# Attention with recurrent memory plus a GELU layer: weight copies kept in PSUM, and the order of VectorE's work in a segment

## Chip, cores and metric

The kernel runs on one core of one Trainium2 chip, as one program. The metric is device time in microseconds of one execution; a lower time is better. Engines are named as in the profile: PE is TensorE, PEld its weight loads, DVE is VectorE, ACT is ScalarE, POOL is GpSimd, and SP is SyncE, which issues most DMAs.

## What is computed

`x` is 2048 tokens of 1024 elements in bf16. After a layer norm it goes two ways, and the output is the sum of x and both:

```python
xn = layernorm(x)
# A: 64 segments of 32 tokens, one after the other, 32 heads of 128, 8 memory rows
for s in range(64):
    h = concat(mem, xn[32*s : 32*s+32])                    # 40 rows
    q, k, v = h @ Wq, h @ Wk, h @ Wv                       # 1024 x 4096 each
    p = softmax(where(mask, q @ k.T / sqrt(128), -1e9))    # per head
    o = (p @ v) @ Wo                                       # 4096 x 1024
    mem, out_A[s] = o[:8], o[8:]
# B: out_B = gelu(xn @ w1 + b1) @ w2 + b2                  # 1024 x 3584 x 1024
out = x + out_A + out_B
```

The mask is causal inside a segment; the 8 memory rows see all and are seen by all. Each segment needs the memory of the one before, so the 64 segments of A are a chain.

## The kernel before

**First stage (lines 293 to 605).** The layer norm and all of B, for four blocks of 512 tokens. During the last block's second product (the loop at line 584) the weights of A are loaded over the weights of B, place by place as each is used for the last time. All these loads are in SP's queue, in program order: an issue that waits for its place holds up those behind it. The line before the last of the stage fetches `xt2` and `xt3`, which must wait until that block's result has been stored from there (line 412); after it stands the load of one half of a Wo unit into `d_oL` (line 605). The other half went into `half_home` early (line 573).

**Second stage (line 612 on).** The weights of A are cut into 64 units of 128 x 2048 bf16 (512 KB): K, Q, V have two halves of eight units each, Wo has sixteen. 46 stay in SBUF for good. 18 must come anew in each segment, through six places (`start_stream`, line 240): when PE has finished a streamed unit (`unit_done`, line 674), the next one in a fixed order is started into its place. 16 of the 18 come by DMA from a packed copy (one of them 384 KB only, with the rest fixed in `part_home`). Two, `IN_PSUM` (the fifth unit of Q's first half) and `IN_BANKS` (the last streamed unit of Wo), are kept in four PSUM banks called `kept`, and DVE copies them out, two banks to a unit (line 247). `keep` (line 647) puts them there once, in segment 0: PE transposes a 128 x 128 block, DVE or ACT copies the result to SBUF, and PE transposes it back into the bank. It uses the bank `mixed` in between.

A segment runs the passes K half 0, Q half 0, K half 1, Q half 1, V half 0, V half 1 (`half_pass`, line 732; eight units, each four matmuls side by side) and then sixteen Wo units (`o_product`). The list `at` puts other work behind a unit of a pass. `scores(u)` (line 808) multiplies queries and keys of half u into the bank `mixed`, ACT takes exponentials, and DVE applies the mask with two minima (line 833). `sums(u)` (line 836) adds the rows up with PE, again in `mixed`; ACT takes a logarithm and two exponentials (lines 852, 855), and DVE makes the weights `pd_main` and `pd_left` (lines 862, 866). `values(u)` multiplies by V. In `turn_q` ACT copies a pass's result to SBUF (line 758) and DVE transposes 32 x 32 blocks (line 772); DVE's order is the order of the program.

**Left rows.** Only memory and the first 24 tokens of a segment go through the passes as its own. The last 8 tokens of four segments are collected in one block of 32 "left" rows. A group's left block is multiplied by one half after another while those units are at hand: by a segment's place in its group of four, left products run in K half 1 and V half 0 (place 0), Q half 0 (place 1), Q half 1 (place 2), K half 0 and V half 1 (place 3), each for the group then beginning or next; Wo's for one place in four. Up to six units of the next left product are made at the end of the segment before. `turn_kL`, `turn_qL`, `left_values` take these results out of PSUM: a copy by DVE, and for K and Q a transpose.
`q_left(u)` (line 788) copies 8 left queries of each head into the block that `scores` reads, from `qL` or, at place 2 and 3 (half 0) and place 3 (half 1), from a piece of the bank `mixed` (`qS`), where `keep_q(u)` (line 798) has saved them at place 1 and 2 before `qL` is overwritten. The masks lie in `mixed` too.

**Banks.** Results of passes, of left products, of `values` and of Wo share three PSUM banks. `new_acc` takes the one that has been free for longest, and PE's first write into it waits for whoever read it last.

Of the kernel before, what the change touches and what calls it, by code (L numbers as in the profile page):

```python
# [10 lines left out]
BF16 = mybir.dt.bfloat16  # L11
U32 = mybir.dt.uint32
F32 = mybir.dt.float32
# [4 lines left out]
P = 128  # L18
# [68 lines left out]
def kernel(  # L87
# [149 lines left out]
    stream_tiles, slot_of = {}, {}  # L237
    used = 0

    def start_stream(slot):  # L240
        if not starts:
            return
        n = starts.popleft()
        unit, t = streams[n], slab(slot)
        if unit in kept_in:
            for c0, bank in kept_in[unit]:
                nc.vector.tensor_copy(out=t[:, c0:c0 + 1024], in_=bank)  # L247
# [45 lines left out]
    with tc.tile_pool(name="ma", bufs=2) as ma, tc.tile_pool(name="mps", bufs=6, space=PSUM) as mps:  # L293
# [191 lines left out]
        for tg in range(4):  # L485
# [46 lines left out]
            if not last:  # L532
                xnT = new_xnT(tg + 1)
                for t in range(4):
                    xtoks[4 * tg + 4 + t] = load_x(4 * tg + 4 + t)
                if tg == 0:
                    for unit, c in copies.items():
                        fetch(c, unit)
                    fetch_resident(*low)
                for t in range(4):  # L540
                    ln_stats(4 * tg + 4 + t, xtoks[4 * tg + 4 + t])
                ln_sqrt(4 * tg + 4, 4 * tg + 8)
                ln_rstd(4 * tg + 4, 4 * tg + 8)
                for t in range(4):
                    ttg = 4 * tg + t
                    xn = ln_apply(ttg + 4)
                    rsb = xtoks[ttg]
                    for nb in range(2):
                        cs = slice(nb * 512, (nb + 1) * 512)
                        ps = mps.tile([P, 512], F32, name="ps")  # L550
                        for fc in range(FC):
                            nc.tensor.matmul(  # L552
                                ps[:, :],
                                lhsT=gts[fc // 4][:, fc % 4, t * P:(t + 1) * P],
                                rhs=w2_sb[fc // 2][:, fc % 2, cs],
                                start=(fc == 0),
                                stop=(fc == FC - 1),
                            )
                        nc.vector.tensor_tensor(out=ps[:, :], in0=ps[:, :], in1=b2bc[:, cs], op=ALU.add)
                        nc.vector.tensor_tensor(out=rsb[:, cs], in0=ps[:, :], in1=rsb[:, cs], op=ALU.add)  # L560
                        if nb == 1:
                            turn_x(ttg + 4, xn, xnT)
                    keep_R(ttg, rsb)
                keep_xT(tg + 1, xnT)
                for t in range(4):
                    turn_R(4 * tg + t)
            else:


                for slot in RING:  # L570
                    start_stream(slot)
                h = 4 * IN_BANKS[1] + 2 * IN_BANKS[2]
                nc.sync.dma_start(out=half_home[:, :], in_=Wo_v[:, h, :])
                fetch_resident(*(place for place in RES_PLACES if place.startswith("w1_")))
                put_mem(o_sb, nxt["hT"], mps.tile([P, 512], F32, name="ps"))
                pss = [mps.tile([P, 512], F32, name="ps") for _ in range(6)]
                pss += [mps.tile([P, 512], F32, name="pT", bufs=2) for _ in range(2)]
                for n in range(8):
                    cs = slice((n % 2) * 512, (n % 2 + 1) * 512)
                    nc.tensor.matmul(pss[n][:, :], lhsT=ones[0:1, :], rhs=b2row[0:1, cs], start=True, stop=False)  # L580
                    nc.tensor.matmul(
                        pss[n][:, :], lhsT=ident, rhs=xtoks[4 * tg + n // 2][:, cs], start=False, stop=False
                    )
                for fc in range(FC):
                    for t in range(4):
                        for nb in range(2):
                            nc.tensor.matmul(  # L587
                                pss[2 * t + nb][:, :],
                                lhsT=gts[fc // 4][:, fc % 4, t * P:(t + 1) * P],
                                rhs=w2_sb[fc // 2][:, fc % 2, nb * 512:nb * 512 + 512],  # L590
                                start=False,
                                stop=(fc == FC - 1),
                            )
                    if fc % 2:
                        fetch_resident(f"w2_{fc // 2}")
                    if fc % 4 == 3:
                        fetch_resident(f"gT{fc // 4}")
                for n in range(8):
                    cs = slice((n % 2) * 512, (n % 2 + 1) * 512)
                    cp = nc.scalar.copy if n % 2 else nc.vector.tensor_copy  # L600
                    cp(out=xtoks[4 * tg + n // 2][:, cs], in_=pss[n][:, :])
                for t in range(4):
                    keep_R(4 * tg + t, xtoks[4 * tg + t])
                fetch_resident("xt2", "xt3")
                nc.sync.dma_start(out=d_oL[:, :], in_=Wo_v[:, h + 1, :])

# [5 lines left out]
    with tc.tile_pool(name="late", bufs=1) as late, \  # L612
# [25 lines left out]
        masks_at = there[:, 32 * NL:32 * NL + NX + GRP * 16]  # L638
        mask_order = masks_at[:, 0:NX]
        mask_left = masks_at[:, NX:].rearrange("p (g q) -> p g q", g=GRP)  # L640
        kept = banks.tile([P, 4, 1024], BF16, name="kept")

        def copy_bits(out, in_):

            nc.vector.tensor_single_scalar(out=out, in_=in_, scalar=0, op=ALU.bitwise_or)

        def keep(unit, c0, w, bank):

            turned = [late.tile([P, 512], BF16, name=f"VL{n}").rearrange("p (k t) -> p k t", k=4) for n in range(2)]
            for n in range(2):  # L650
                for k in range(4):
                    nc.tensor.transpose(trs[n][:, k, :], w[:, 512 * n + P * k:512 * n + P * (k + 1)], ident)
                (nc.scalar.copy if n else nc.vector.tensor_copy)(out=turned[n], in_=trs[n])
            for n in range(2):
                for k in range(4):
                    c1 = 512 * n + P * k
                    nc.tensor.transpose(kept[:, bank, c1:c1 + P], turned[n][:, k, :], ident)
            kept_in.setdefault(unit, []).append((c0, kept[:, bank, :]))

        def unit_tile(unit):  # L660
# [29 lines left out]
        for s in range(NSEG):  # L690
# [87 lines left out]
            def turn_kL(ps, u):  # L778
                kL[u] = sp.tile([P, 16, 32], BF16, name=f"kL{u}")
                turn(ps, kL[u][:, :, :], nc.vector.tensor_copy)  # L780
# [133 lines left out]
                        )  # L914


            psK, psKL = half_pass("K", 0, left_k[0], {})
            turn_k(psK, 0)
            if first:
                turn_kL(psKL, 0)  # L920
            psQ, psQL = half_pass("Q", 0, left_q[0], {})
            if first:
                keep(IN_BANKS, 1024, d_oL, 2)
                keep(IN_BANKS, 0, half_home, 3)
                nc.sync.dma_start(out=part_home, in_=Wo_v[:, 4 * PART[1] + 2 * PART[2], 0:PART_COLS])
                copy_bits(mixed[:, 468:512].bitcast(U32), mask.bitcast(U32))
                for t in outs:
                    nc.vector.memset(t[:, :, 0:32], 0.0)
                turn_qL(psQL, 0)
            q_left(0)  # L930
            turn_q(psQ)
            if left_q[0] and not first:
                keep_q(0)
                turn_qL(psQL, 0)
            psK1, psK1L = half_pass("K", 1, left_k[1], {})
            st["kT", 1] = nat_home
            rows_out(psK1, nat_home, nc.scalar.copy)
            at = {
                0: [lambda: scores(0), lambda: nc.vector.transpose(out=nat_home, in_=nat_home)],
                7: [lambda: sums(0)],  # L940
            }
            if left_k[1]:
                at[1] = [lambda: turn_kL(psK1L, 1)]
            elif left_k[0]:
                at[1] = [lambda: turn_kL(psKL, 0)]
            psQ1, psQ1L = half_pass("Q", 1, left_q[1], at)
            if first:
                turn_qL(psQ1L, 1)
            q_left(1)
            turn_q(psQ1)  # L950
            if left_q[1] and not first:
                keep_q(1)
                turn_qL(psQ1L, 1)
            psV, psVL = half_pass("V", 0, left_v[0], {})
            st["V", 0] = values_out(psV, sp.tile([P, 512], BF16, name="v", tag="a"), nc.scalar.copy)
# [27 lines left out]
            else:  # L983
                at = {5: [lambda: values(1, (0, 1))]}
            if left_v[1] and not first:
                at[6].append(lambda: left_values(1, psV1L))
            at.setdefault(0, []).append(load_res)
            psX = new_acc()
            for n, unit in enumerate(O_UNITS):
# [103 lines left out]
```

## Time and profile before

| what | value |
|---|---|
| four runs | 1893.39, 1894.7, 1905.26, 1908.27 us; median 1899.98 |
| the profiled execution | 1908.27 us, of which the span from first to last instruction is 1906.6 |
| PE, DVE, ACT, POOL busy | 91%, 48%, 33%, 14% |
| segment 0 begins, ends | 423.4 us (first product of K), 466.0 us (copy of its Wo result, line 1002) |
| segments 1 to 63 | 466.0 to about 1890 us, 22.6 us each |
| HBM read over the span | 599.39 MB |

The page's times are those of one execution, so sums are made against 1908.27 us. "Idle before" in a group's line is the time its engine stood still just ahead of it, with who ended that. A matmul's end is modelled, so a gap read between two matmuls is some 0.2 us shorter than the pause in issuing them. In a view by windows the columns are the stretch, its length, each engine's busy time, PE's granted clock, the mean busy share of the DMA engines (it can exceed 1 a little, since packets of one engine overlap) and GB/s.

### The profile page before, as it was taken

Reading aid. Unit: us, or ns where it says so; the run is one execution under the profiler, and the core shown is the slowest. Engines: PE = TensorE matmul, PEld = TensorE weight load, DVE = VectorE, ACT = ScalarE, POOL = GpSimd, SP = SyncE. Lnnn points to the kernel's source line nnn. Section 1 sums busy time; section 2 is a strip of 40 time slices with the busy share of each in tenths; the row PEclk is TensorE's granted clock in tenths of the full one; section 3 lists DMA queues with packets and bytes.
Section 4 is the critical chain, followed back from the end, with each engine's and each line's share of the span. In section 5 each row is a group of like instructions: output and inputs, shape, how many; then the busy total and the mean of one; then the engine's idle time right before and its main releaser. Section 6 shows DMA issues by size and latency. Waiting matters only on the chain.

```text
span 1906.6 us, 72995 instructions
## 1 busy us (share of the span) xinstructions
PE 1737.0 (91%) x32255; PEld 944.9 (50%) x32275; DVE 921.7 (48%) x2222; ACT 637.0 (33%) x1356; POOL 276.1 (14%) x538
## 2 busy tenths in 40 slices
PE   7999999997899899999989889989899999999887
PEld 3444444444454555545445545454555455555454
DVE  6657574604444444444444444444445444444443
ACT  5334342402333333333323333333333333333332
POOL 0000000001341111211112111112111111111211
PEclk9999999999999999999999999999999999999999
DMA  9821211588999999999999999999999999999997
GB/s 335 265 52 44 55 45 52 189 327 315 399 388 387 364 380 391 383 377 397 374 378 371 382 366 370 378 368 380 372 397 378 385 385 385 361 369 386 369 369 303
DMA packets 220025, 618.39 MB, mean 324 GB/s; under 512 B 47243, under 2 KB 65595, under 8 KB 219708
## 3 DMA queue, kind: packets, MB, share of 16 engines
q1 hardware_dynamic: 199292, 593.57, 82.3%
q0 software_dynamic: 16320, 17.52, 2.8%
q8 instruction: 252, 4.13, 0.8%
q10 hardware_dynamic: 4096, 2.64, 0.4%
q14 instruction: 65, 0.53, 0.1%
HBM read 599.39 MB, written 30.34 MB: 330 GB/s over the span
## 4 chain that ended last, share of the span: by engine, by line
PE 67%; DMA 19%; DVE 6%; issue 4%; ACT 3%; POOL 0%; DVEq 0%; ACTq 0%; POOLq 0%; SPq 0%
PE acc L714 32%; PE ps L503 10%; DMA u<-Wc_K 10%; PE acc L907 9%; PE ps L552 8%; DMA u<-Wc_O 5%; PE ps L587 2%; DMA u<-Wc_Q 2%; PE acc L881 2%; ACT mixed L855 2%; DVE b_oL L772 1%; DMA outL_d<-half_home 1%; DVE pd_main L862 1%; PE mixed L816 1%; DMA u<-Wc_V 1%
## 5 line engine op out<-in xcount | busy, mean ns | idle before, releaser
L714 PE MATMUL acc<-u,hr_home 128*32 128x512 bf16 x11520 | 784.5, 382 | 36.3 <-DMA u<-Wc_K 14.3
L714 PEld LDWEIGHTS <-hr_home 128*32 128x32 bf16 x12288 | 354.7, 97 | 326.5 <-issue 77.8
L714 PE MATMUL acc<-u,hrL 128*32 128x512 bf16 x2880 | 260.2, 380 | 17.4 <-issue 9.6
L503 PE MATMUL ps<-u 128*128 128x512 bf16 x896 | 196.4, 382 | 2.6 <-ACT u L387 2.6
L907 PE MATMUL acc<-u,d_oL 128*32 128x256 bf16 (+1 forms) x3552 | 177.1, 290 | 15.3 <-DMA u<-Wc_O 8.1
L247 DVE COPY u<-kept 128x1024 bf16<-128x1024 bf16 x254 | 163.4, 685 | 28.4 <-PE acc L907 12.3
L907 PEld LDWEIGHTS <-b_oL 128*32 128x32 bf16 (+1 forms) x3552 | 110.9, 98 | 75.9 <-issue 44.0
L552 PE MATMUL ps<-u 128*128 128x512 bf16 x657 | 146.2, 379 | 0.8
L503 PEld LDWEIGHTS <-u 128*128 128x128 bf16 x896 | 88.3, 99 | 109.4 <-issue 4.3
L907 PEld LDWEIGHTS <-d_oL 128*32 128x32 bf16 (+1 forms) x3552 | 104.0, 98 | 66.5 <-issue 24.8
L862 DVE TENSOR_TENSOR pd_main<-half_home,mixed 128x320 bf16<-128x320 bf16 x128 | 62.4, 488 | 146.7 <-ACT mixed L855 142.8
L714 PEld LDWEIGHTS <-hrL 128*32 128x32 bf16 x3072 | 92.3, 96 | 72.8 <-issue 30.5
L907 PE MATMUL acc<-u,b_oL 128*32 128x256 bf16 (+1 forms) x1665 | 108.9, 290 | 19.3 <-DMA u<-Wc_O 8.8
L772 DVE STREAM_TRANSPOSE b_oL<-b_oL 128x512 bf16<-128x512 bf16 x128 | 90.6, 708 | 67.7 <-ACT b_oL L758 67.7
L907 PE MATMUL acc<-W_O,b_oL 128*32 128x256 bf16 (+1 forms) x1776 | 109.9, 289 | 6.5 <-issue 6.5
L758 ACT CAST kT<-acc 128x512 bf16<-128x512 f32 x64 | 37.4, 585 | 229.5 <-PE acc L714 229.5
L259 POOL DMA_DIRECT2D hr_home<-hr_d x58 | 32.6, 562 | 547.5 <-PE acc L714 547.5
L552 PEld LDWEIGHTS <-u 128*128 128x128 bf16 x672 | 65.3, 98 | 77.3 <-DVE g_u L519 0.4
L758 ACT CAST b_oL<-acc 128x512 bf16<-128x512 f32 x128 | 75.2, 587 | 81.5 <-PE acc L714 81.5
L1002 ACT CAST d_oL<-acc 128x256 bf16<-128x256 f32 (+1 forms) x63 | 26.9, 426 | 217.4 <-PE acc L907 217.4
L833 DVE TENSOR_TENSOR half_home<-half_home,mixed 128x96 bf16<-128x96 bf16 (+1 forms) x256 | 37.6, 187 | 127.9 <-ACT half_home L828 127.9
L511 ACT ACTIVATE g_xb<-ps,b1col 128x512 bf16<-128x512 f32 x112 | 76.8, 686 | 61.3 <-PE ps L503 60.2
(129 smaller groups left out, 2062.9 us busy)
## 6 DMA issues: line engine op xcount, KB each, us to landing
u<-Wc_K SPq DMA_DIRECT2D x320, 512.0 KB
u<-Wc_V SPq DMA_DIRECT2D x256, 512.0 KB
u<-Wc_O SPq DMA_DIRECT2D x256, 512.0 KB
u<-Wc_Q SPq DMA_DIRECT2D x128, 512.0 KB
u<-Wc_O SPq DMA_DIRECT2D x64, 384.0 KB
u<-in_B_w_dram SPq DMA_DIRECT2D x14, 512.0 KB
u<-in_A_Wq_dram SPq DMA_DIRECT2D x14, 512.0 KB
u<-in_A_Wv_dram SPq DMA_DIRECT2D x12, 512.0 KB
```

What stands on the lines that cost most here:

```text
L247: nc.vector.tensor_copy(out=t[:, c0:c0 + 1024], in_=bank)
L503: nc.tensor.matmul(ps[:, :].rearrange("p (s t) -> p s t", t=SEG), lhsT=w1_sb[fb // 14 * 8 + kt][:, (fb % 14) * P:(fb % 14 + 1) * P], rhs=x ...
L511: nc.scalar.activation(out=xb[:, :], in_=ps[:, :], func=ACT.Identity, bias=b1col[:, fb:fb + 1], scale=1.0)
L552: nc.tensor.matmul(ps[:, :], lhsT=gts[fc // 4][:, fc % 4, t * P:(t + 1) * P], rhs=w2_sb[fc // 2][:, fc % 2, cs], start=(fc == 0), stop=(fc ...
L587: nc.tensor.matmul(pss[2 * t + nb][:, :], lhsT=gts[fc // 4][:, fc % 4, t * P:(t + 1) * P], rhs=w2_sb[fc // 2][:, fc % 2, nb * 512:nb * 512 ...
L714: nc.tensor.matmul(o, lhsT=lhs[:, i, :], rhs=m, start=(i == seq[0]), stop=(i == seq[-1]), tile_position=(0, 32 * j),)
L758: cp(out=out, in_=ps.rearrange("p (h e) -> p h e", e=32))
L772: nc.vector.transpose(out=home, in_=home)
L855: nc.scalar.activation(out=mixed[:, 160 * b:160 * b + 160], in_=mixed[:, 0:160], func=ACT.Exp, scale=-1.0, bias=off[:, b:b + 1],)
L862: nc.vector.tensor_tensor(out=pdA.rearrange("p c b q -> p b c q"), in0=prA[:, None, :, :].to_broadcast([P, 2, 4, 40]), in1=dd, op=ALU.mult,)
L881: nc.tensor.matmul(oV[r][:, c, :, :], lhsT=V[q, c * P:(c + 1) * P], rhs=pdA[q, c, :, :], start=(c == 0), stop=False, skip_group_check=True ...
L907: nc.tensor.matmul(acc[r:r + n // 8, 0:n], lhsT=lhs[:, 4 * (i % 4) + 2 * u + k, :], rhs=w_t[:, c0:c0 + n], start=(unit == O_UNITS[0] and k ...
```

## The change

It has five parts.

- **Words.** `kept` becomes four banks of 512 f32. `keep` is one DVE instruction, an OR with 0 on 32-bit words, from SBUF into the bank; PE and ACT have no part in it. The copy out (line 247) becomes the same instruction on 512 words in place of a copy of 1024 bf16.
- **Segment 0.** The load of `d_oL` is issued ahead of the last product of B. The two `keep`s of `IN_BANKS`, the DMA into `part_home`, the copy of the masks into `mixed` and two memsets move from behind the first Q pass to the start of the segment.
- **Left queries.** In segments after the first, `q_left(u)` runs behind unit 1 of Q's pass of half u, and `keep_q(u)` behind unit 2; before, both stood after the pass.
- **Sums.** `sums(0)` runs behind unit 6 of Q half 1 instead of unit 7.
- **Left K and V.** At place 3 `turn_kL(.., 0)` moves from behind unit 1 of Q half 1 to after that pass's `turn_q`; `left_values(1)` moves from behind Wo unit 6 to Wo unit 9.

```diff
+    def copy_bits(out, in_):
+
+        nc.vector.tensor_single_scalar(out=out, in_=in_, scalar=0, op=ALU.bitwise_or)
...
             for c0, bank in kept_in[unit]:
-                nc.vector.tensor_copy(out=t[:, c0:c0 + 1024], in_=bank)
+                copy_bits(t[:, c0:c0 + 1024].bitcast(U32), bank.bitcast(U32))
...
                 put_mem(o_sb, nxt["hT"], mps.tile([P, 512], F32, name="ps"))
+                nc.sync.dma_start(out=d_oL[:, :], in_=Wo_v[:, h + 1, :])
...
                 fetch_resident("xt2", "xt3")
-                nc.sync.dma_start(out=d_oL[:, :], in_=Wo_v[:, h + 1, :])
...
-        kept = banks.tile([P, 4, 1024], BF16, name="kept")
+        kept = banks.tile([P, 4, 512], F32, name="kept")
...
         def keep(unit, c0, w, bank):
 
-            turned = [late.tile([P, 512], BF16, name=f"VL{n}").rearrange("p (k t) -> p k t", k=4) for n in range(2)]
-            for n in range(2):
-                for k in range(4):
-                    nc.tensor.transpose(trs[n][:, k, :], w[:, 512 * n + P * k:512 * n + P * (k + 1)], ident)
-                (nc.scalar.copy if n else nc.vector.tensor_copy)(out=turned[n], in_=trs[n])
-            for n in range(2):
-                for k in range(4):
-                    c1 = 512 * n + P * k
-                    nc.tensor.transpose(kept[:, bank, c1:c1 + P], turned[n][:, k, :], ident)
+            copy_bits(kept[:, bank, :].bitcast(U32), w.bitcast(U32))
             kept_in.setdefault(unit, []).append((c0, kept[:, bank, :]))
...
+            if first:
+                keep(IN_BANKS, 1024, d_oL, 2)
+                keep(IN_BANKS, 0, half_home[:, :], 3)
+                nc.sync.dma_start(out=part_home, in_=Wo_v[:, 4 * PART[1] + 2 * PART[2], 0:PART_COLS])
+                copy_bits(mixed[:, 468:512].bitcast(U32), mask.bitcast(U32))
+                for t in outs:
+                    nc.vector.memset(t[:, :, 0:32], 0.0)
             psK, psKL = half_pass("K", 0, left_k[0], {})
             turn_k(psK, 0)
             if first:
                 turn_kL(psKL, 0)
-            psQ, psQL = half_pass("Q", 0, left_q[0], {})
+            at = {} if first else {1: [lambda: q_left(0)]}
+            if left_q[0] and not first:
+                at[2] = [lambda: keep_q(0)]
+            psQ, psQL = half_pass("Q", 0, left_q[0], at)
             if first:
-                keep(IN_BANKS, 1024, d_oL, 2)
-                keep(IN_BANKS, 0, half_home, 3)
-                nc.sync.dma_start(out=part_home, in_=Wo_v[:, 4 * PART[1] + 2 * PART[2], 0:PART_COLS])
-                copy_bits(mixed[:, 468:512].bitcast(U32), mask.bitcast(U32))
-                for t in outs:
-                    nc.vector.memset(t[:, :, 0:32], 0.0)
                 turn_qL(psQL, 0)
-            q_left(0)
+                q_left(0)
             turn_q(psQ)
             if left_q[0] and not first:
-                keep_q(0)
                 turn_qL(psQL, 0)
...
             at = {
                 0: [lambda: scores(0), lambda: nc.vector.transpose(out=nat_home, in_=nat_home)],
-                7: [lambda: sums(0)],
+                6: [lambda: sums(0)],
             }
+            if not first:
+                at[1] = [lambda: q_left(1)]
+                if left_q[1]:
+                    at[2] = [lambda: keep_q(1)]
             if left_k[1]:
-                at[1] = [lambda: turn_kL(psK1L, 1)]
-            elif left_k[0]:
-                at[1] = [lambda: turn_kL(psKL, 0)]
+                at.setdefault(1, []).append(lambda: turn_kL(psK1L, 1))
             psQ1, psQ1L = half_pass("Q", 1, left_q[1], at)
             if first:
                 turn_qL(psQ1L, 1)
-            q_left(1)
+                q_left(1)
             turn_q(psQ1)
+            if left_k[0] and not first:
+                turn_kL(psKL, 0)
             if left_q[1] and not first:
-                keep_q(1)
                 turn_qL(psQ1L, 1)
...
             if left_v[1] and not first:
-                at[6].append(lambda: left_values(1, psV1L))
+                at[9] = [lambda: left_values(1, psV1L)]
```

More of the change, by code (lines that the diff above doesn't have):

```diff
@@ L640 @@
         mask_left = masks_at[:, NX:].rearrange("p (g q) -> p g q", g=GRP)
-        kept = banks.tile([P, 4, 1024], BF16, name="kept")
-        def copy_bits(out, in_):
-            nc.vector.tensor_single_scalar(out=out, in_=in_, scalar=0, op=ALU.bitwise_or)
+        kept = banks.tile([P, 4, 512], F32, name="kept")
         def keep(unit, c0, w, bank):
-            turned = [late.tile([P, 512], BF16, name=f"VL{n}").rearrange("p (k t) -> p k t", k=4) for n in range(2)]
-            for n in range(2):
-                for k in range(4):
-                    nc.tensor.transpose(trs[n][:, k, :], w[:, 512 * n + P * k:512 * n + P * (k + 1)], ident)
-                (nc.scalar.copy if n else nc.vector.tensor_copy)(out=turned[n], in_=trs[n])
-            for n in range(2):
-                for k in range(4):
-                    c1 = 512 * n + P * k
-                    nc.tensor.transpose(kept[:, bank, c1:c1 + P], turned[n][:, k, :], ident)
+            copy_bits(kept[:, bank, :].bitcast(U32), w.bitcast(U32))
             kept_in.setdefault(unit, []).append((c0, kept[:, bank, :]))
```

## The prediction

> **What bounds the kernel now.** I read the slices of the page first, then the view by windows, then who ended PE's idle time at the lines that the change touches, then VectorE's order in time in single segments.
>
> ```profile
> PE 1737.0 (91%) x32255; PEld 944.9 (50%) x32275; DVE 921.7 (48%) x2222; ACT 637.0 (33%) x1356; POOL 276.1 (14%) x538
> DMA  9821211588999999999999999999999999999997
> ```
>
> ```profile
> 430.00:435.00 5.00, 3.04 (x45) 2.04 (x48) 0.84 (x2) 1.17 (x2) 0.00 (x0) 1.00 0.71 219
> 435.00:440.00 5.00, 2.42 (x36) 1.52 (x29) 0.85 (x2) 0.58 (x1) 0.00 (x0) 1.00 0.95 331
> ...
> 450.00:455.00 5.00, 2.66 (x52) 1.31 (x52) 2.81 (x6) 1.52 (x4) 0.00 (x0) 1.00 0.55 206
> 455.00:460.00 5.00, 4.74 (x127) 2.40 (x120) 1.49 (x4) 1.55 (x4) 0.00 (x0) 1.00 0.61 202
> 460.00:465.00 5.00, 4.95 (x148) 3.85 (x141) 2.71 (x6) 1.79 (x5) 0.71 (x1) 1.00 0.85 258
> ...
> 500.00:1800.00 1300.00, 1176.47 (x27112) 671.95 (x27108) 611.42 (x1447) 420.20 (x974) 233.20 (x436) 1.00 0.99 379
> ```
>
> The reader is to see two regimes. From 500 us on the DMA engines are 0.99 busy and PE is busy for 1176 of 1300 us: both are nearly full, so neither alone sets the time. In segment 0 (423 to 466 us) neither is full.
>
> ```profile
>   DVE b_oL L772: 18.4, 30
>   DVE mixed L645: 9.0, 14
> ```
>
> These, of line 816, are PE's idle time ahead of the scores. All the waits listed below are for half 1, in V half 1 behind unit 0. At place 1 and 3 PE waits for the transposed queries (14 times and 12 times in 500 to 1800 us, 0.6 us each), at place 2 for `keep_q`, which stands behind that transpose.
>
> ```profile
> 1320.55 0.70 DVE L772 STREAM_TRANSPOSE b_oL<-b_oL 128x512 bf16<-128x512 bf16 x1
> 1321.18 0.20 DVE L645 TENSOR_SCALAR mixed<-qL_last 128x64 uint32<-128x64 uint32 x1
> ...
> 1321.43 0.20 PE L816 MATMUL mixed<-b_oL,d_oL 128*32 128x40 bf16 x4 [0.65 <-DVE mixed L645]
> ```
>
> This is a segment of place 2. The scores start 0.05 us after `keep_q` ends (1321.38), not after the transpose (1321.25), though `keep_q` writes columns 340 to 403 of `mixed` and the scores columns 0 to 223. So PE's writes to this bank wait for VectorE's write to other columns of it. That decides what the early copies cost.
>
> ```profile
> 1063.01 0.30 DVE L833 TENSOR_TENSOR half_home<-half_home,mixed 128x96 bf16<-128x96 bf16 x2 [1.29 <-ACT half_home L828]
> 1063.23 0.70 DVE L939 STREAM_TRANSPOSE d_oL<-d_oL 128x512 bf16<-128x512 bf16 x1
> 1063.86 0.65 DVE L758 CAST kL<-acc 128x512 bf16<-128x512 f32 x1
> ...
> 1063.81 0.26 PE L841 MATMUL mixed<-half_home,small_consts 128*32 128x160 bf16 x4
> ...
> 1066.81 0.20 PE L816 MATMUL mixed<-b_oL,d_oL 128*32 128x40 bf16 x4 [0.55 <-DVE b_oL L772]
> ```
>
> This is place 3: minima, transpose of K, cast and transpose of left K on VectorE, sums on PE at 1063.81, scores of half 1 at 1066.81.
>
> **Words, copy out.** 254 copies.
>
> ```profile
> L247 DVE COPY u<-kept 128x1024 bf16<-128x1024 bf16 x254 | 163.4, 685 | 28.4 <-PE acc L907 12.3 <-PE acc L714 9.0 <-DMA u<-Wc_O 2.8
> L645 DVE TENSOR_SCALAR mixed<-qL 128x128 uint32<-128x128 uint32 x15 | 4.0, 267 | 0.0
> L645 DVE TENSOR_SCALAR mixed<-qL_last 128x64 uint32<-128x64 uint32 x15 | 3.0, 199 | 0.0
> ```
>
> The OR on words costs 267 ns for 128 and 199 for 64, so 1.06 ns a word and 131 fixed: 675 ns for 512 words. Those rows write PSUM; reading 512 f32 from PSUM costs 652 ns (cast of kL) to 688 (cast of VL). Bounds: 417 ns (512 bf16 from PSUM, line 387) and 699 ns (line 559, 512 f32); I take 680, nothing. At 417 ns it would be 68 us of VectorE, of which only the waits for this copy lie on the path: 6.6 us on PE's matmuls, 2.3 on its loads.
>
> The Trainium skill speaks for more: "VectorE: DVE Perf Modes", in the section on the TRN2 errata, says that reading bf16 as 32-bit integers halves the time of a copy; 254 copies would then save 82 us of VectorE. The section "Why PSUM operands drop a tier" of that page speaks against it: from PSUM a 16-bit copy may go at two a cycle and a 32-bit one at one, which gives nothing. The trace's 685 ns for 1024 bf16, beside 652 for 512 f32, agrees with the second.
>
> **Segment 0.** PE leaves Q's pass for `keep` twice: 429.56 to 434.12 and, with a 0.96 us wait for `d_oL`, 435.60 to 441.19: 10.2 us. In exchange VectorE gets four instructions of about 675 ns: two ahead of K's pass, where it is idle until 427.48, two behind Q's unit 4, hidden by three units of 0.43 us and the next cast. PE can't use 10.2 us: SP stands until 432.5 behind `xt2` and `xt3`, whose wait for the store is untouched, so the first streamed unit of Q half 1 lands some 4 us later, at 437. From there DMA sets the pace. The DMA engines' idle time from 430 to 470 us is 5 x (0.29 + 0.05 + 0.45 + 0.39 + 0.15 + 0.04) = 6.9 us; the first 1.5 stays. So -5.4 us; bounds 0 and -10.2. The earlier `d_oL` load (256 KB, 0.7 us of DMA) goes ahead of the fetches behind it in SP's queue, and waits for `put_mem`'s matmuls at 365.4, which are past by then. DMA has room after it (share 0.62 to 0.88 from 405 to 425 us), so nothing; without room 0.7. `part_home` no longer waits in SP's queue for PE (439.25).
>
> **Steady segments.** What hangs behind `sums(0)`: 1.5 us after it ACT's exponentials are done, then pd_main, pd_left, `q_left` (0.1 visible), transpose. All of it moves by one unit of PE, 0.215 us.
>
> *Place 1*: -0.215 for the sums and -0.1 for `q_left`: scores of half 1 at -0.3 us. `keep_q` goes into Q half 0, where no write to `mixed` waits for it.
>
> *Place 2*: VectorE's order in Q half 1 is now minima, K's transpose, `q_left(1)`, `keep_q(1)`, and the sums write the bank that `keep_q` writes. By place 3's times with its casts left out: transpose ends 1063.93, `q_left` 1064.05, `keep_q` 1064.17, sums at 1064.23 where they were at 1063.81: +0.4 us, with seven products in place of eight made before. The chain then lacks `q_left` (0.1) and `keep_q` (0.12): scores at +0.2. Where ACT's exponentials come late (they wait for a store from the same place 10 times, 11.1 us in all) +0.9. I take +0.4; bounds -0.45 (no such wait) and +0.9.
>
> *Place 3*: `q_left(1)` reads saved queries from `mixed`. Whether PE's write waits for a read of other columns, no row shows; if so, sums at 1064.14, +0.33; if not -0.2. More certain is the second wait. Replaying the order in which the three banks come free, V half 1's left product now gets the bank of left K, whose cast stands behind the transpose of Q. That ends at 1066.6 to 1067.05, the cast 0.65 later, then the left unit, 0.215: scores at 1067.5 to 1067.9 instead of 1066.81, +0.7 to +1.0. On the other side `left_values` at Wo unit 9 lets `IN_BANKS` pass: 8.9 us of waits for line 247 in 15 such segments, -0.6. I take +0.4; bounds -0.35 and +1.0.
>
> *Place 0*: left K's cast falls behind `q_left`, and V half 0's left product already waits 0.25 us for it: +0.14.
>
> Sum of a group: -0.3 + 0.4 + 0.4 + 0.14 = +0.64 us, in 15 groups +9.6. Of that none comes through if DMA sets the pace, all if PE does; with both above 90% I take half, +4.8. With -5.4 the sum is about -0.6: 1908.27 becomes 1907.7, and the median, 8.3 lower than the profiled execution, 1899.
>
> **Rivals.** *The waits are gone and nothing takes their place.* PE waits 18.4 + 9.0 us ahead of the scores, 8.9 for the copies, 2.5 for the cast of left queries: 38.8 us, half of it 19.4, and 5.4 at the start: 1875. For it speaks that each edit points at one of these rows; against it the bank wait above and the order of banks.
>
> *PE waits inside Q half 1.* The bank `mixed` is held by VectorE's copies when the sums come: place 2 +0.9, place 3 +1.0, and no half: 15 x (0.9 + 1.0 + 0.14 - 0.3) = 26 us, less 5.4: 1920. It decides from the point where PE rather than DMA sets the pace. For it speaks PE's 91%, against it the DMA share of 0.99.
>
> *Words copy at twice the speed.* Only the 8.9 us are on the path, so about 1895: it can't be told from my forecast.
>
> **How the numbers follow.** 1% (19 us) is about what a measurement of this kernel tells from no change; the four runs spread over 15. The forecast, with its unknown bounds and the copy's speed, lies within it: 0.77. The first rival has 0.13 and the second 0.10. The range goes from 1884 (half of the first rival's gain beyond the forecast's) to 1914 (place 2 and 3 at their upper bounds, two thirds of it coming through).
>
> **What would show it.** Copies out at 675 to 690 ns. No transposes at lines 652 and 657; K half 1 beginning near 431 us instead of 441 and segment 0 ending near 458 to 460. Sums at line 841 waiting for line 645's OR at place 2, and perhaps for `q_left` at place 3. Left products of V (line 714, hrL) waiting about 1 us for the cast of kL. No wait of Wo's products for the copies. If the sums wait for nothing and PE's idle time at line 816 falls below 10 us, the first rival is right; if segment 0 ends no earlier, my start is wrong.

## The result, and the profile after

The changed kernel takes 1888.96 us (median of 53 runs, 1873.61 to 1902.26); the kernel before took 1896.05 us beside it (79 runs, 1880.23 to 1914.09). The ratio is 0.9965, with a 95% interval of 0.9954 to 0.9977: 6.6 us faster (4.4 to 8.7), 0.35%. The forecast was within 1%, with 0.6 us by the sum; 1888.96 lies inside its range of 1884 to 1914.

The page's lines of the engines and of DMA in 40 slices, after:

```profile
PE 1726.0 (91%) x32191; PEld 930.8 (49%) x32211; DVE 918.3 (49%) x2222; ACT 634.7 (34%) x1352; POOL 276.1 (15%) x538
...
DMA  9821211499999999999999999999999999999998
```

The tenth slice, in which segment 0 runs, has gone from 8 to 9. By windows, with the same columns as before:

```profile
430.00:435.00 5.00, 4.42 (x85) 2.36 (x80) 3.18 (x6) 0.58 (x1) 0.00 (x0) 1.00 0.68 212
435.00:440.00 5.00, 1.95 (x64) 1.02 (x59) 2.21 (x5) 0.94 (x2) 0.00 (x0) 1.00 0.92 322
...
450.00:455.00 5.00, 4.88 (x112) 2.79 (x104) 1.78 (x4) 1.93 (x5) 0.71 (x1) 1.00 1.03 409
455.00:460.00 5.00, 4.37 (x124) 2.97 (x124) 1.69 (x3) 0.80 (x2) 0.00 (x0) 1.00 1.05 405
...
500.00:1800.00 1300.00, 1177.05 (x27216) 666.21 (x27212) 608.66 (x1447) 419.60 (x972) 230.62 (x432) 1.00 1.00 381
```

Between 450 and 460 us DMA moves 409 and 405 GB/s where it moved 206 and 202. From 500 us on nothing stands out: 1177 us of PE instead of 1176, 381 GB/s instead of 379.

The groups of instructions after, for the copy out, V's and the other left products, the sums and the scores of half 1:

```profile
L242 DVE TENSOR_SCALAR u<-kept 128x512 uint32<-128x512 uint32 x254 | 163.3, 685 | 24.9 <-PE acc L899 10.3 <-PE acc L706 6.2 <-DMA u<-Wc_O 5.5
L706 PE MATMUL acc<-u,hrL 128*32 128x512 bf16 x2880 | 253.8, 379 | 25.5 <-DVE kL L750 18.1 <-issue 3.7 <-DVE qL_last L750 1.9
L833 PE MATMUL mixed<-half_home,small_consts 128*32 128x160 bf16 x512 | 33.3, 236 | 18.6 <-DVE mixed L242 13.0 <-DVE b_oL L786 4.4 <-issue 0.7
L808 PE MATMUL mixed<-b_oL,d_oL 128*32 128x40 bf16 x1024 | 24.5, 181 | 11.0 <-DVE b_oL L764 8.5 <-issue 2.3
```

The last three of these groups before (lines 714, 841 and 816 there):

```profile
L714 PE MATMUL acc<-u,hrL 128*32 128x512 bf16 x2880 | 260.2, 380 | 17.4 <-issue 9.6 <-DVE kL L758 2.9 <-DVE qL_last L758 2.3
L841 PE MATMUL mixed<-half_home,small_consts 128*32 128x160 bf16 x512 | 33.5, 234 | 1.2 <-DVE half_home L833 0.6 <-issue 0.6
L816 PE MATMUL mixed<-b_oL,d_oL 128*32 128x40 bf16 x1024 | 24.2, 181 | 27.4 <-DVE b_oL L772 18.4 <-DVE mixed L645 9.0
```

The reader is to see a wait that changed its place. Ahead of the scores 16.4 us have gone (27.4 to 11.0); ahead of the sums 17.4 have come (1.2 to 18.6), and 8.1 ahead of the left products (17.4 to 25.5). The copy out takes 685 ns, to the nanosecond what it took.

The timeline of the kernel after shows both new waits. A segment of place 2:

```profile
1307.08 0.70 DVE L934 STREAM_TRANSPOSE d_oL<-d_oL 128x512 bf16<-128x512 bf16 x1
1307.71 0.15 DVE L786 COPY b_oL<-qL_last 128x128 bf16<-128x128 bf16 x1
1307.78 0.22 DVE L242 TENSOR_SCALAR mixed<-qL_last 128x64 uint32<-128x64 uint32 x1
1308.05 0.25 PE L833 MATMUL mixed<-half_home,small_consts 128*32 128x160 bf16 x4 [0.53 <-DVE mixed L242]
```

and one of place 3:

```profile
1055.99 0.19 DVE L786 COPY b_oL<-mixed 128x128 bf16<-128x128 bf16 x1
1056.23 0.25 PE L833 MATMUL mixed<-half_home,small_consts 128*32 128x160 bf16 x4 [0.31 <-DVE b_oL L786]
...
1058.34 0.70 DVE L764 STREAM_TRANSPOSE b_oL<-b_oL 128x512 bf16<-128x512 bf16 x1
...
1058.97 0.65 DVE L750 CAST kL<-acc 128x512 bf16<-128x512 f32 x1
...
1059.67 0.40 PE L706 MATMUL acc<-u,hrL 128*32 128x512 bf16 x4 [0.77 <-DVE kL L750]
```

At place 2 the sums stand behind K's transpose, `q_left` and `keep_q`. At place 3 they stand behind `q_left`'s read of `mixed`, and V's left product behind the cast of left K, which stands behind the transpose of Q.

### The profile page after: what moved, and what is told of

Its sections match the earlier page's. It is cut to its first block, busy times and chain, and to the rows that moved or that the text cites. A ratio compares the mean times of both kernels' runs of the same rounds, so it can differ in the third digit from the quotient of the medians.

```text
span 1890.5 us, 72836 instructions
## 1 busy us (share of the span) xinstructions
PE 1726.0 (91%) x32191; PEld 930.8 (49%) x32211; DVE 918.3 (49%) x2222; ACT 634.7 (34%) x1352; POOL 276.1 (15%) x538
## 5 line engine op out<-in xcount | busy, mean ns | idle before, releaser
L706 PEld LDWEIGHTS <-hr_home 128*32 128x32 bf16 x12288 | 344.0, 96 | 320.3 <-issue 65.7
L706 PE MATMUL acc<-u,hrL 128*32 128x512 bf16 x2880 | 253.8, 379 | 25.5 <-DVE kL L750 18.1
L899 PE MATMUL acc<-u,d_oL 128*32 128x256 bf16 (+1 forms) x3552 | 177.0, 290 | 16.6 <-DMA u<-Wc_O 10.1
L242 DVE TENSOR_SCALAR u<-kept 128x512 uint32<-128x512 uint32 x254 | 163.3, 685 | 24.9 <-PE acc L899 10.3
L1000 ACT CAST d_oL<-acc 128x256 bf16<-128x256 f32 (+1 forms) x63 | 26.9, 426 | 216.8 <-PE acc L899 216.8
```

Source lines behind the costliest of these rows:

```text
L706: nc.tensor.matmul(o, lhsT=lhs[:, i, :], rhs=m, start=(i == seq[0]), stop=(i == seq[-1]), tile_position=(0, 32 * j),)
L899: nc.tensor.matmul(acc[r:r + n // 8, 0:n], lhsT=lhs[:, 4 * (i % 4) + 2 * u + k, :], rhs=w_t[:, c0:c0 + n], start=(unit == O_UNITS[0] and k ...
L1000: nc.scalar.copy(out=o_sb[:, 0:no, :], in_=psX[:, 0:32 * no].rearrange("p (h e) -> p h e", e=32))
```

## The experiments

Theory A: the start of segment 0 carries the gain, and the steady part brings about as much wait as it removes. Theory B: the terms of the prediction, -5.4 for the start and +4.8 for the rest. Theory C: the steady part gains. All ratios are to the kernel before, with 95% intervals; the change itself has 0.9965 (0.9954 to 0.9977).

**e1, the start alone.** The steady order of before, put into the changed kernel:

```diff
-            at = {} if first else {1: [lambda: q_left(0)]}
-            if left_q[0] and not first:
-                at[2] = [lambda: keep_q(0)]
-            psQ, psQL = half_pass("Q", 0, left_q[0], at)
+            psQ, psQL = half_pass("Q", 0, left_q[0], {})
...
-                6: [lambda: sums(0)],
+                7: [lambda: sums(0)],
...
+            elif left_k[0]:
+                at[1] = [lambda: turn_kL(psKL, 0)]
...
-                at[9] = [lambda: left_values(1, psV1L)]
+                at[6].append(lambda: left_values(1, psV1L))
```

> The change without its steady part: words in kept and copied out, keep put ahead of K half 0 in segment 0, d_oL fetched early; the order of q_left, keep_q, sums, the casts of left K and left V is that of before. Theory A (the start carries the gain and the steady part gives nearly nothing): 6 to 7.5 us faster than before, so within 1 us of the whole change (6.6 faster). Theory B (my terms as written: start -5.4, steady part +4.8): 5 to 6 faster than before, yet the whole change would then have to be near 0, so this run would stand 4 to 6 us below the whole change's time only if the start is worth 11. Theory C (the steady part carries the gain, since it removes waits ahead of the scores): 0 to 3 us faster than before.

Measured: 0.995 (0.9923 to 0.9977), 9.5 us faster (4.4 to 14.6).

**e2, the steady part alone.** The reverse: the kernel before with only these parts of the diff.

```diff
-            psQ, psQL = half_pass("Q", 0, left_q[0], {})
+            at = {} if first else {1: [lambda: q_left(0)]}
+            if left_q[0] and not first:
+                at[2] = [lambda: keep_q(0)]
+            psQ, psQL = half_pass("Q", 0, left_q[0], at)
...
-                7: [lambda: sums(0)],
+                6: [lambda: sums(0)],
...
-                at[6].append(lambda: left_values(1, psV1L))
+                at[9] = [lambda: left_values(1, psV1L)]
```

> Before with only the steady part: q_left and keep_q early in the Q passes, sums at unit 6, left K cast behind turn_q at place 3, left V cast at Wo unit 9; keep still goes over TensorE inside Q half 0 of segment 0 and the copies out are bf16. Theory A: within 1.5 us of before. Theory B: 4 to 6 us slower than before. Theory C: 4 to 7 us faster. The waits of the sums for keep_q at place 2 (0.9 us each) and of V's left product for the cast of left K at place 3 (1 us each) should be in this trace as in that of the whole change, whatever the time.

Measured: 0.9995 (0.9966 to 1.0025). Both waits are there as in the whole change: 11.9 us of the sums for `keep_q` at place 2, 14.7 us of V's left product for left K at place 3. C falls with e1, which gains at least 4.4 us without the steady part. B's +4.8 lies just above e2's interval (-6.5 to +4.7 us), but the whole change less e1 is +2.8 us (-2.7 to +8.4), which leaves room for it, so B isn't excluded. A fits both: the start gives the gain, and the steady part nothing that can be told from zero.

**e3, left K of place 3 early again.**

```diff
+            elif left_k[0]:
+                at.setdefault(1, []).append(lambda: turn_kL(psKL, 0))
...
-            if left_k[0] and not first:
-                turn_kL(psKL, 0)
```

> The change, but at place 3 left K is cast and transposed at unit 1 of Q half 1 as before. V half 1's left product should no longer wait for that cast (14.4 us in 15 such segments), sums of place 3 stand some 1.3 us behind two more VectorE instructions again. If half of PE's waits come through: 4 to 7 us faster than the whole change. If DMA sets the pace: within 2 us of it.

Measured: 0.9924 (0.9892 to 0.9956), 7.8 us below the whole change. PE's idle time ahead of the left products falls from 25.5 to 11.4 us, the wait of the sums stays (19.8).

**e4, the sums at unit 7 again.**

```diff
-                6: [lambda: sums(0)],
+                7: [lambda: sums(0)],
```

> The change, but the sums of half 0 stand at unit 7 of Q half 1, as before. The wait of the sums for keep_q at place 2 (12.6 us in 14 segments) and for q_left at place 3 (4.4) should shrink by some 0.2 us each, one unit of PE without a left one, 0.43 with one, while what hangs behind the sums moves later by the same. If PE's waits come through by half: 0 to 3 us faster than the whole change; if DMA sets the pace: within 1.5 us. Should it be over 3 us slower, the earlier sums carry a gain that I put at 0.2 us a segment.

Measured: 0.9959 (0.9931 to 0.9987), 1 us from the whole change (within some 6 either way). The wait of the sums halves (18.6 to 9.3 us), and that of the scores behind them grows from 11.0 to 16.2: a unit earlier or later only moves the wait between these two places.

**e5, `keep_q` of place 2 in Q half 0.**

```diff
             if left_q[0] and not first:
                 at[2] = [lambda: keep_q(0)]
+            if left_q[1] and not first:
+                at[4] = [lambda: keep_q(1)]
...
-                if left_q[1]:
-                    at[2] = [lambda: keep_q(1)]
```

> The change, but at place 2 keep_q stands in Q half 0 (unit 4) instead of Q half 1 (unit 2). If it is the write of keep_q to the bank of the sums that PE waits for, the wait at place 2 (0.9 us each, 12.6 us in 14 segments) is gone and segments of place 2 last 22.0 us, as before the change, instead of 22.3: with all of the 0.3 us coming through 15 x 0.3 = 4.5 us faster than the whole change, with half of the wait coming through 6.5. If DMA sets the pace, within 1.5 us of the whole change. Should the wait stay, it was for q_left or the transpose, not for keep_q.

Measured: 0.994 (0.9915 to 0.9965), 4.7 us below the whole change, with intervals that overlap. The timeline of the same segment of place 2 settles who was waited for:

```profile
1306.50 0.70 DVE L936 STREAM_TRANSPOSE d_oL<-d_oL 128x512 bf16<-128x512 bf16 x1
1306.64 0.25 PE L833 MATMUL mixed<-half_home,small_consts 128*32 128x160 bf16 x4
...
1307.12 0.15 DVE L786 COPY b_oL<-qL_last 128x128 bf16<-128x128 bf16 x1
```

The sums now start while the transpose is running, and wait for nothing. In the whole trace the 13.0 us that they waited for `keep_q` are gone.

**e6, all three waits out.** e3 and e5 together, and `q_left(1)` directly behind the scores:

```diff
-                at[1] = [lambda: q_left(1)]
+                at[0].insert(1, lambda: q_left(1))
```

> The change with left K of place 3 turned at unit 1 of Q half 1 (as before), keep_q of place 2 in Q half 0, and q_left of half 1 ahead of the transpose of K half 1 on VectorE, while ScalarE makes the exponentials. None of the three waits that the steady part brought (sums for keep_q, sums for q_left, V's left product for the cast of left K) should be left. If the waits that I put into my sum at +0.4 at place 2 and +0.4 at place 3 are what the steady part costs: 8 to 14 us faster than the whole change, about 15 to 20 faster than before, groups of four segments at 89.7 us instead of 90.55. If DMA sets the pace: within 3 us of the whole change.

Measured: 0.9885 (0.9851 to 0.992), 1875.5 us. A second time (e12, with e9 and e10):

> e6 once more, to compare with e9 and e10 on the same chip: 19 to 23 us faster than before (ratio 0.988 to 0.990), as in its first run.

Measured: 0.9891 (0.9858 to 0.9924), 1876.87 us. These intervals lie wholly below that of the change. The same three groups in e6:

```profile
L706 PE MATMUL acc<-u,hrL 128*32 128x512 bf16 x2880 | 257.3, 384 | 11.4 <-DVE kL L750 4.7 <-issue 2.7 <-DVE qL_last L750 1.9
...
L833 PE MATMUL mixed<-half_home,small_consts 128*32 128x160 bf16 x512 | 33.6, 234 | 2.4 <-DVE half_home L825 2.2
...
L808 PE MATMUL mixed<-b_oL,d_oL 128*32 128x40 bf16 x1024 | 24.3, 181 | 14.4 <-DVE b_oL L764 13.3 <-issue 0.7
```

Together 28.2 us of idle time instead of 55.1. For these 26.9 us the time falls by 15.2 (0.9965 less 0.9885) and 14.0 us, so a little over half of a removed wait comes through. This version beats both kernels.

**e7, words in the old place.** In segment 0 the copies into PSUM go back behind Q half 0, and the load of `d_oL` back to the end of the first stage:

```diff
-                nc.sync.dma_start(out=d_oL[:, :], in_=Wo_v[:, h + 1, :])
...
                 fetch_resident("xt2", "xt3")
+                nc.sync.dma_start(out=d_oL[:, :], in_=Wo_v[:, h + 1, :])
...
-            if first:
-                keep(IN_BANKS, 1024, d_oL, 2)
-                keep(IN_BANKS, 0, half_home[:, :], 3)
...
             if first:
+                keep(IN_BANKS, 1024, d_oL, 2)
+                keep(IN_BANKS, 0, half_home[:, :], 3)
...
                 turn_qL(psQL, 0)
                 q_left(0)
```

> The change, but in segment 0 the copies into PSUM, the copy of the mask and the memsets stand behind Q half 0 as before, and d_oL is fetched last: what is left of the start is that VectorE's words take the place of the transposes on TensorE. If TensorE's 10.2 us are what the start gains: segment 0 shorter than before by 5 to 7 us, and all within 2 us of the whole change. If it is the earlier place and fetch: K half 1 waits for VectorE's queue or for d_oL, segment 0 shorter by 0 to 3 us, and 4 to 7 us slower than the whole change.

Measured: 0.9986 (0.9959 to 1.0013). Its timeline in segment 0:

```profile
432.62 0.46 SPq L609 DMA_DIRECT2D d_oL<-in_A_Wo_dram  x1
...
436.98 0.69 DVE L242 TENSOR_SCALAR kept<-d_oL 128x512 uint32<-128x512 uint32 x1 [6.22 <-DMA d_oL<-in_A_Wo_dram]
...
439.70 0.62 PE L706 MATMUL acc<-u,hrL 128*32 128x512 bf16 x4 [8.63 <-DVE qL L750]
```

PE makes no transposes any more. K half 1 begins at 430.67, but its first left product only at 439.70, 2.5 us sooner than before (442.24): PE waits 8.63 us for the cast of left Q, which stands on VectorE behind the copy of `d_oL`, and that waits for a load that SP could only issue at 432.62, behind `xt2` and `xt3`. In this wait and behind it PE's granted clock is low, 0.50 from 435 to 440 us and 0.51 from 440 to 444, and the next ten products follow one another at 0.43 us instead of 0.215, some 2 us more (an estimate from these two figures).

**e11, early load, old place.** The second half of e7's edit alone: the copies go back behind Q half 0, and the load of `d_oL` stays early.

> The change with the copies into PSUM, the mask and the memsets behind Q half 0 of segment 0 as before, but d_oL fetched early as in the change. With e7 (late fetch as well, 1896 where before is 1896, K half 1 at 439.7) it tells the early fetch from the early place. If the fetch carries it: K half 1 begins near 433.5 (two copies of 0.68 and the small ones ahead of the cast of left Q), hidden by the wait for the first streamed unit of Q half 1, and the time is within 2 us of the whole change. If the early place carries it: within 2 us of e7, 5 us above the whole change.

Measured: 0.9929 (0.9897 to 0.996). Its timeline:

```profile
426.47 0.69 DVE L242 TENSOR_SCALAR kept<-d_oL 128x512 uint32<-128x512 uint32 x1
427.20 0.69 DVE L242 TENSOR_SCALAR kept<-half_home 128x512 uint32<-128x512 uint32 x1
...
429.18 0.40 PE L706 MATMUL acc<-u,hrL 128*32 128x512 bf16 x4 [2.45 <-DVE qL L750]
```

This execution's first stage ended 4.6 us sooner than that of the change, so stretches are compared, from the cast of K half 0 in segment 0 to that in segment 1: 43.3 us before, 41.8 in e7, 35.3 in e11, 35.7 in the whole change. The ten profiles with the change's start spread from 35.7 to 39.8 us there (e6 36.6, e12, the same kernel, 39.8), and e2, with the old one, has 45.5. So e7's 1.5 us less than before can't be told from nothing, while the 6.5 between e7 and e11 are more than this spread. The old place costs K half 1's first left product a wait of 2.45 us instead of 0.58. The 2.80 us that the change then waits for the first streamed unit of Q half 1 don't occur in e11, so the old place costs nothing that is seen here; the load is what counts. What the early load gains with PE's transposes left in was not run.

**e8, more work on PE.** Four extra products at the start of Q half 0 in each segment but the first, which the product itself then overwrites:

```diff
+                    for _ in range(4 if (w, i, u) == ("Q", 0, 0) and not first else 0):
+                        product(w, i, t, hT, ps, [0])
                     product(w, i, t, hT, ps, range(KT))
```

> The change with the first main product of Q half 0 made four times more in each segment but the first: 4 x 0.215 = 0.86 us more of TensorE in 63 segments, 54 us, with nothing more to load. It measures what share of a microsecond on PE comes through to the end, which I took at a half. If DMA sets the pace: 0 to 10 us slower than the whole change. If half: 20 to 34. If PE sets it: 45 to 54.

Measured: 1.0183 (1.0143 to 1.0223): 41 us (33 to 49) above the change for 63 x 0.86 = 54 us, so 0.76 of it comes through (0.62 to 0.91). The view by windows:

```profile
500.00:1800.00 1300.00, 1193.58 (x27399) 672.05 (x27391) 593.27 (x1413) 410.34 (x951) 225.90 (x422) 1.00 0.99 371
```

In the same stretch DMA moves 371 GB/s at a share of 0.99, where before moved 379 at 0.99 and e6 moves 383 at 1.00. A busy share of 0.99 did not mean that DMA could go no faster.

**e9, left V cast at Wo unit 6**, in e6:

```diff
-                at[9] = [lambda: left_values(1, psV1L)]
+                at[6].append(lambda: left_values(1, psV1L))
```

> The kernel without the three waits (e6), with left V of half 1 cast at Wo unit 6 as before the change instead of unit 9. It tells what that edit is worth by itself: I put it at -0.6 us a segment of place 3, since Wo's products no longer wait for the kept unit's copy behind that cast (8.9 us of such waits before). If so, Wo's products wait again for VectorE's copy out (6 to 9 us in 15 segments) and this kernel is 4 to 7 us slower than e6 of the same call; if DMA covers it, within 2 us.

Measured: 0.9887 (0.9851 to 0.9922), beside 0.9891 for e6. Groups of Wo's products, in e9 and then in e6:

```profile
L899 PE MATMUL acc<-u,b_oL 128*32 128x256 bf16 (+1 forms) x1665 | 108.9, 290 | 31.4 <-DMA u<-Wc_O 18.1 <-DVE u L242 8.2 <-issue 4.8
```

```profile
L899 PE MATMUL acc<-u,b_oL 128*32 128x256 bf16 (+1 forms) x1665 | 108.2, 290 | 17.9 <-DMA u<-Wc_O 12.1 <-issue 4.0
```

The waits for the copy come back (8.2 us), and the time does not show them. With intervals of this width a cost of 5 us isn't excluded.

**e10, the scores of half 1 one unit later**, in e6 (the values of half 0 stay at unit 1, behind them):

```diff
-            at = {0: [lambda: scores(1)], 4: [lambda: sums(1)]}
+            at = {1: [lambda: scores(1)], 5: [lambda: sums(1)]}
```

> e6 with the scores of half 1 one unit later in V half 1 (unit 1 instead of 0) and its sums at unit 5 instead of 4: PE fills the wait for the transpose of Q half 1 (0.36 us each at places 1 and 3, some 10 us in 28 segments) with a unit of 0.215 us, 0.43 with a left one. By the share that e8 showed (41 of 54 us) 4 to 8 us faster than e6; if the values of half 0 or what hangs behind the sums is late next, 0 to 5 us slower.

Measured: 0.9888 (0.9851 to 0.9925), no gain beside e6. PE's idle time ahead of the scores does fall, from 14.4 us in e6 and 16.6 in e12 to 3.3. Where it went isn't shown: ahead of the sums 2.3 us have come (4.7 instead of 2.4), and ahead of the streamed Wo units stand 43.3 us, where the two executions of e6's kernel have 37.1 and 42.5.

## Why the prediction was right, and where it was off

The forecast "within 1%" held, and so did nearly every mechanism. What was off is the sum: its two large terms were to cancel and did not. That the time lies inside the range owes something to the range's width of 30 us: the median was to be 1899 and is 10 us lower, of which 4 are the kernel before itself (1899.98 in four runs, 1896.05 in 79) and 6 the sum. By the working given for them the range's ends would be 1887 (half of 24.2 below 1899.4) and 1912 (17.4 less 5.4 above 1899.98), a little nearer than 1884 and 1914; 1888.96 lies inside these too. For the steps between, here are medians over the 13 or 14 segments of a place from 538 to about 1760 us, counted from the first scores of the segment (worked out from the traces' times, us):

| | sums, half 0 | scores, half 1 | Wo begins | Wo's last product | next cast of K |
|---|---|---|---|---|---|
| place 1, before | 1.81 | 4.78 | 7.42 | 14.74 | 18.56 |
| place 1, after | 1.54 | 4.41 | 7.48 | 14.82 | 18.65 |
| place 2, before | 2.39 | 5.49 | 8.22 | 14.38 | 18.58 |
| place 2, after | 2.71 | 5.58 | 8.11 | 14.72 | 18.85 |
| place 3, before | 1.92 | 4.92 | 9.67 | 15.18 | 19.14 |
| place 3, after | 2.04 | 5.70 | 10.15 | 14.78 | 18.71 |
| place 3, e6 | 1.54 | 4.57 | 8.93 | 14.35 | 18.31 |

Two executions of one kernel (e6 and e12) differ by up to 0.4 us in such medians from Wo's last product on, so differences of this size in the last two columns are not told from none.

- **Words out: right.** 685 ns beside 685; 680 was taken. The Trainium skill's page "VectorE: DVE Perf Modes" has both rules that were weighed. The tip in its section on the TRN2 errata, to copy bf16 as 32-bit integers in half the time, isn't seen in these 254 copies out of PSUM. Its section "Why PSUM operands drop a tier" agrees with them.
- **Segment 0: mechanism right, size a little small, cause half named.** K half 1 was to begin near 431 instead of 441 and did at 430.90 instead of 441.19; the first streamed unit of Q half 1 was to land near 437, and PE waited for it until 439.18; the segment was to end at 458 to 460 and did at 458.85, 7.1 us sooner, where -5.4 stood in the sum. The 10.2 us were put down to PE's transposes, and the early load of `d_oL` was listed at "nothing". In e7, without this load, segment 0 is 1.5 us shorter (43.3 to 41.8), less than executions differ by, and in e11, with it, 8.0. PE's waits in e7 show why: the load's wait took the place of the transposes.
- **Place 0: the wait right, its effect not seen.** V half 0's left product waits 0.34 us for left K (3.75 us in 11 segments) where it waited 0.24, near the +0.14 forecast, but the scores of half 1 stand at 6.12 instead of 6.16 (medians over the same stretch).
- **Place 1: right.** Scores at -0.37; -0.3 was forecast.
- **Place 2: right.** Sums at +0.32 (forecast +0.4), scores at +0.09 (+0.2); the sums wait for the OR on words, 12.6 us in 14 segments.
- **Place 3: the waits right, the net wrong.** "Whether PE's write waits for a read of other columns" is answered: it does, 4.4 us in 14 segments, 0.31 each (0.33 was the price for that case). V's left product waits 0.96 us for left K (14.4 us in 15), and the scores come 0.78 later (0.7 to 1.0). But the +0.4 that was taken for the segment is not there. Wo begins 0.48 later and its last product comes 0.40 sooner: 4.63 us from first to last instead of 5.51. The 0.6 taken off for left V is too small for these 0.88, and left V is only part of it. In the 13 segments of place 3 before, PE's waits of over 0.1 us ahead of Wo's products are 5.7 us for the copy out and 5.2 in which the profile shows nothing that was waited for; after, they are 1.6 and none. The first part is left V's: in e9, which casts it at unit 6 again, 7.8 us of waits for the copy are there, where e6 has 0.8. The second goes with the late cast of left K: with that cast early again, in e6, 4.7 us of it are back, and Wo, 1.22 sooner, takes 5.42. That a later PE finds more ready would explain it, but isn't shown.
- **The sum: this is the step that was off.** It gave -0.6, and -6.6 (-8.7 to -4.4) was measured. The start's -5.4 is too small by 1.7 us in the profile of segment 0 (7.1) and by 4.1 in e1 (9.5, with 5.4 inside its interval). Of the steady part's "+0.64 us, in 15 groups +9.6" half, +4.8, was to come through. e2 has -0.9 (-6.5 to +4.7), the whole change less the 7.1 us of segment 0 leaves +0.5, and the whole change less e1 +2.8 (-2.7 to +8.4). The first speaks against +4.8 and the last leaves room for it, so how the 6 us divide between the two terms isn't settled. The share itself wasn't too high: e6 shows a little over half for removed waits, e8 0.76 for added work on PE. A likely reason is that the shift of the scores was summed, and not that of the segment's end, 14 us later, with a Wo pass between that was 0.88 us shorter at place 3.
- **Rivals.** PE waits inside Q half 1 as the second rival said, but not at its price. "The waits are gone and nothing takes their place", 1875, is not what the change does; e6 comes near it, at 1875.5 and 1876.87, which is 21.8 and 20.7 us below the kernel before where that rival had 24.8. "Words copy at twice the speed" falls with the 685 ns.

What stays open: e3 shows that left K's new place costs 7.8 us (with intervals that leave room from about 1 to 14), so something in the steady part must give a like amount back. The earlier sums do not, as far as e4 can tell. Left V's later cast takes away the waits for the copy that e9 brings back (8.2 us), but the time of e9 doesn't show it. Whether the early `q_left` at place 1 or the later arrival at Wo gives the rest was not told apart.

PE's granted clock is a further candidate. Its mean is 0.9951 over 54 runs of the change and 0.9931 over 67 of the kernel before; among the runs of before, a clock 0.001 higher goes with 2.2 to 2.5 us less, so these 0.002 would be 4 to 5 of the 6.6 us. It isn't what gives e1 its gain (0.9924, with 0.9929 for the runs of before beside it); e2, with the steady order, has 0.9940 beside the same 0.9929. Compared at the same clock (a fit over all runs, 2.0 us per 0.001), e1 stands 11 us below the kernel before, e2 2 above and the change 5 below. The start would then be worth twice its term, and the steady part may cost what the sum said. Whether the order of the work raises the clock or these runs merely had a higher one is not shown.

## What to carry to other kernels

In a program whose waits go by bank, as here, a small copy into or out of a PSUM bank belongs in a pass in which PE doesn't write that bank, whatever its columns: making one such copy two passes earlier ended a wait of 0.9 us in one segment of four. Before a cast that frees a bank is moved back, count which product gets that bank next in the rotation. And when an engine's work is taken off a path, look at the load that it was working on: here the transposes hid a DMA that came just as late, and taking them away without moving that DMA's issue (e7) brought no gain that could be told from zero.

## What the runs showed of the hardware

- In this program PE's writes to a PSUM bank wait for VectorE's reads of other columns of it as well as for its writes: 0.31 us for `q_left`, which reads from column 340 on while the sums write columns 0 to 159. The Trainium skill has the rule behind this, "PSUM — Partial Sum Buffer", section "PSUM bank collisions raise a hardware error": two engines on one bank and the same 32 partitions must be kept apart by bank, not by address, reads included. The waits seen here agree with it; that the chip needs them was not tried.
- The time at which segment 0 starts has two values: the first cast of K stands at 426.4 to 427.0 us in seven of the fourteen profiles and at 422.4 to 423.1 in the other seven. Among the eleven that load `d_oL` early, whose first stage is the same, four have the later value and seven the earlier; the three that load it late all have the later one. Single profiled spans therefore differ by 4 us before the changed part begins.
- PE's granted clock falls to 0.50 for stretches of 3.41 us, four to five times between 500 and 1880 us in the profiles before and after, and once for 10.24 us in e7, around its wait of 8.63 us. In e7 the products follow one another at 0.43 us there instead of 0.215. One stretch of 3.41 us lowers the mean clock of such an execution by 0.0009 (half of 3.41 in some 1890 us).
